# Reordering the attention half of a fused adaLN, linear-attention and GeGLU kernel

## The chip, the cores and the metric

The kernel runs on one core of a Trainium2 chip. The metric is the device time of one execution in microseconds; the time before the change is the median of three runs, 790.18 us (786.46 to 790.93). One execution was also recorded by the hardware profiler; its span is 788.5 us, and all the views below are of that one.

## The reference

The input x has 2048 rows (tokens) of 1024. Six modulation vectors come from a condition c. Then come a linear attention with 32 heads of 32 and a gated feed-forward part with an inner width of 3584:

```python
mod = (_silu(c) @ w_mod).reshape(c.shape[0], 6, 1, -1)
sa, ca, ga, sb, cb, gb = (mod[:, 0], mod[:, 1], mod[:, 2], mod[:, 3], mod[:, 4], mod[:, 5])
h = _layernorm(x) * (1 + ca) + sa
q, k, v = h @ wqkv                      # split in 32 heads of 32
phi = lambda t: where(t > 0, t + 1, exp(t)) + 1e-6
kv = einsum('bhsd,bhse->bhde', phi(k), v)
z = sum over s of phi(k)
o = einsum('bhqd,bhde->bhqe', phi(q), kv) / (einsum('bhqd,bhd->bhq', phi(q), z) + 1e-6)
x = x + ga * (o @ wo)
h = _layernorm(x) * (1 + cb) + sb
x = x + gb * ((gelu(h @ w_gate) * (h @ w_up)) @ w_down)
```

## The kernel before, in words

The rows are cut into four blocks of 512 (four tiles of 128 rows each). The kernel keeps its operands transposed, with the contracted dimension on the 128 partitions, so each block's normalised rows are stored to a scratch in HBM (`xa_scr`) and come back through a transposing load (line 593); then eight VectorE instructions (line 595) apply scale and shift. Block 0 is transposed on TensorE instead.

The products for V, Q, gate, up and down are computed with seven in place of eight half-size products (the scheme that Strassen and Winograd made known). It needs sums of operand halves, which VectorE makes beforehand (`h_sum` line 598, `w_sum` line 605, `h2_sums` line 913), and combinations of partial results afterwards. `seven` (line 629) gives the seven stages s1 to s7 of V or Q; each is 8 matmuls of 128x128 by 512 columns. The partial sums of s1, s3, s5 and s6 share two banks of the accumulator memory (`QA`), those of s2, s4 and s7 two others (`QB`). K is a plain product in groups of 8 matmuls (`k_group`, line 749), with `phi` behind each.

The attention has a linear form, so keys and values are reduced to one matrix per head. `kv_products` (line 760) multiplies a block's phi(k) with its V and its ones column, in three groups of up to three 128-wide slices (kb = 0, 1, 2); VectorE adds each to `kvzacc`. For blocks 0 to 2 all three groups are in bank 6. At the end `kv_matrix` (line 795) makes the block-diagonal matrices. `wp_step` (line 785) folds them into the output weight: Wp = KV times (Wo times ga). `den_start` (line 774) makes the denominators of one slice of 512 rows on TensorE, its reciprocal by Ln and Exp on ScalarE, and the returned function multiplies phi(q) by it on VectorE; there are 32 of those.

`ModSet` (line 465) computes the modulation vectors, in three sets of two. A set has eight `step`s, each of four 32-row matmuls on one 512 KB piece of w_mod; then `columns` copies the row out of the accumulator (line 493), turns it into columns with four small matmuls (line 498) and copies those (line 500); `spread` copies a vector over all partitions with two matmuls (line 506). These use banks 6 and 7 in turn.

`kvq_phase` writes TensorE's order out by hand: `blocks[b]` is a list of K groups, V stages and Q stages, and `put(b, i, ...)` hangs other work at position i of block b. A K group does the hung work after its matmuls; a V or Q stage does it before them. Q works on a pair of blocks at a time and on a quarter of the columns per seven stages: `Q[pr, j]`. `wo_phase` (line 936) holds the last Q stages, the Wp steps and the denominators, and then the 16 output tiles (`wo_tile`, line 922: 16 matmuls, two additions of x, and a store of the new x to `x2_scr`). The first eight tiles are layer-normed at once (`ln2_stats`, `ln2_xhat`) and come back through two transposing loads (line 901) as the operand of the first feed-forward half; `h2_mod` (line 908) scales and shifts them. `gate_up(g)` and `down_out(g)` do the feed-forward part for each half of the rows (g = 0, 1).

Every call is recorded by `Plan` and issued at the end. TensorE keeps the order of the program. The order of VectorE, ScalarE, GpSimd and the SyncE queue, which issues all loads, comes from `Plan.order`: it simulates the program forward with assumed costs, picking by due times, simulates it backward to get new due times, repeats this from two starts, and keeps the best. Each engine and the SyncE queue then does its work in that order: an instruction that waits holds up all that stand behind it. Buffers are written out by hand as offsets in one big tile; rings (`Ring`) hand out their slots in turn, and a write into a slot waits for the last readers of that memory.

Of the kernel before, what the change touches and what calls it, by code (L numbers as in the profile page):

```python
# [20 lines left out]
class Op:  # L21
    __slots__ = ("eng", "fn", "args", "kw", "line", "cost", "bytes", "table", "preds", "succs", "due", "ready", "wait",
                 "start", "done", "n")


class Plan:

    LINE = 16

# [44 lines left out]
    def add(self, eng, name, args, kw, line):  # L74
        op = Op()
        op.n, op.eng, op.fn, op.args, op.kw, op.line = len(self.ops), eng, name, args, kw, line
        op.preds, op.succs, op.bytes, op.table = set(), set(), 0, None
# [28 lines left out]
    def cost(self, op, outs, ins):  # L106
# [8 lines left out]
        elif op.fn.startswith("dma"):  # L115
            a = outs[0]
            op.cost, op.bytes = 1000 if op.eng == "POOL" else 60, math.prod(d[1] for d in a.ap) * (4 if a.dtype == FP32 else 2)
            if op.fn == "dma_start_transpose":
                op.bytes = 3584 * 360
# [16 lines left out]
    SYNC = 120  # L136
    DMA_LATENCY = 1500
    GBPS = 360
    AHEAD = 15000
    ROUNDS = 6  # L140

    def sweep(self, back, key):
# [12 lines left out]
        while left:  # L155
            best = None
            for e in self.engines:
# [5 lines left out]
                else:  # L163
                    if not avail[e]:
                        continue
                    when = lambda o: o.ready if back or not o.bytes else max(o.ready, o.due - self.AHEAD)
# [10 lines left out]
            if op.bytes:  # L177
                bw = max(bw, op.done) + op.bytes / self.GBPS
                op.done = bw + self.DMA_LATENCY
# [5 lines left out]
            for s in op.preds if back else op.succs:  # L185
                o = ops[s]
                o.wait -= 1
                o.ready = max(o.ready, op.done + (0 if o.eng == op.eng and not op.bytes else self.SYNC))
# [3 lines left out]

    def slack(self):
        t, ideal = 0.0, {}
        for op in self.ops:
            if op.eng == "PE":
                ideal[op.n] = t
                t += op.cost
        for op in reversed(self.ops):
            dur = op.cost + (self.DMA_LATENCY + op.bytes / self.GBPS if op.bytes else 0)  # L200
            due = min((self.ops[s].due - self.SYNC for s in op.succs), default=t + 20000.0) - dur
            op.due = min(due, ideal[op.n]) if op.eng == "PE" else due

    def order(self):
# [8 lines left out]
        def backward():  # L213
            t = self.sweep(True, lambda o: (-o.due, -o.n))
            for op in self.ops:
                op.due = t - op.done

        for rounds in (1, 3):
            if rounds == 1:
                self.slack()  # L220
            else:
                for op in self.ops:
                    op.due = op.n
            forward()
            if rounds == 3:
                for op in self.ops:
                    op.due = op.start
            for i in range(rounds):
                backward()
                forward()  # L230
                for op in self.ops:
                    op.due = op.start
        return [self.ops[n] for _, n in best[1]]
# [13 lines left out]
def kernel(  # L247
# [130 lines left out]
    wm0_ring.slots += Ring(170, [MW], BF16, 1).slots  # L378
# [6 lines left out]
    pqT = [pq2[0][:, 0], pq2[0][:, 1], pq2[1][:, 1], pq2[1][:, 0]]  # L385
    h12 = [at(104, [2, KD, TG], F16), at(136, [2, KD, TG], F16)]
    hr1 = [h12[0][:, 0], h12[0][:, 1], h12[1][:, 1], h12[1][:, 0]]
    WvT = at(120, [3, KH, NW], F16)
    Wp = at(120, [KD, D], F16)
    Sab = [at(152, [2, 3, KH, HB], F16), at(158, [2, 3, KH, HB], F16)]  # L390
    Sb = [Sab[0][:, 0], Sab[0][:, 1], Sab[1][:, 1], Sab[1][:, 0]]
    wm_ring = Ring(195.25, [MW], BF16, 2)
    qf_ring = Ring(170, [TG], FP32, 6)
    Wo_sb = at(11.75, [KD, D], BF16)
    phe_ring = Ring(182, [TG], F16, 3)
    phr_ring = Ring(185, [TG], F16, 3)
# [6 lines left out]
    bst_ring = Ring(205, [NBN, nc.vector.BN_STATS_DIM], FP32, 4)  # L403
# [20 lines left out]
    xio_ring = Ring(183, [NW], BF16, 6)  # L424
# [349 lines left out]
    def den_start(b, g):  # L774
# [3 lines left out]
        ac.activation(out=lnd, in_=psd, func=AF.Ln, bias=eps6, scale=1.0)  # L778
        rden = rden_ring()
# [27 lines left out]
    def kvq_phase():  # L807
# [32 lines left out]
        k, v = kk[1], V[1]  # L840
        blocks.append([k[0], k[1], v[0], k[2], v[1], k[3], v[2], k[4], v[3], k[5], v[4], k[6], v[5], k[7], v[6]])
        k, v, q = kk[2], V[2], Q[0, 0] + Q[0, 2]
# [93 lines left out]
    def wo_phase(last):  # L936
        dens = []
        for i in range(4):
            last[i](())
            for f in dens:  # L940
                f()
# [269 lines left out]
```

## Time and profile before

| | us | share of the span |
|---|---|---|
| span of the profiled run | 788.5 | |
| TensorE matmul busy (PE) | 761.5 | 97% |
| TensorE weight load busy (PEld) | 343.5 | 44% |
| VectorE busy (DVE) | 567.7 | 72% |
| ScalarE busy (ACT) | 330.1 | 42% |
| GpSimd busy (POOL) | 54.0 | 7% |
| mean traffic of HBM | 154 GB/s | |
| first matmul | at 4.87 | |
| first gate and up matmul (line 1003) | at 275.76 | |
| last VectorE instruction begins | at 785.34 | |

A line of a group of instructions names its line in the kernel, the engine, the operation, the output and input with their shapes, and a count; after the first bar come the busy time and the mean duration in ns, after the second the time for which the engine stood idle just before, and what ended it. A line of the waits names the instruction that waited, then what it waited for, the total, how often, and the longest. "PE psum L754 <- DVE mem L595" is TensorE's matmul of line 754 waiting for the VectorE instruction of line 595. The duration of one matmul in the trace includes its way through the array; the pace of a stream of matmuls is read from one start to the next.

### The profile page before, as it was taken

To read this page: it belongs to the slowest core of one execution; us is meant where nothing else is said; L and a number is where in the kernel's file an instruction comes from. 1 tells how busy PE (TensorE), PEld (TensorE's weight loads), DVE (VectorE), ACT (ScalarE), POOL (GpSimd) and SP (SyncE) were. 2 spreads that over 40 slices of the span, in tenths; PEclk is the share of its full clock that TensorE was granted. 3 is DMA by queue.
4 is the path that set the end of the run, shared out by engine and by line. 5 is a ranking of instruction groups with operands and counts; after the bars stand their busy time and mean duration, and the time that the engine had idled before them with its cause. 6 is when DMAs were issued, how large, how long until landed. Compare 5 with 4: busy or idle time off the path is not lost.

```text
span 788.5 us, 10345 instructions
## 1 busy us (share of the span) xinstructions
PE 761.5 (97%) x3666; PEld 343.5 (44%) x3666; DVE 567.7 (72%) x1145; ACT 330.1 (42%) x575; POOL 54.0 (7%) x120
## 2 busy tenths in 40 slices
PE   5989998999999999999999999999999999999997
PEld 2434443444344444444444444444444444444443
DVE  4996756748997987788897677597777677646144
ACT  1764645846994055454445301004454454530000
POOL 1221200000034100000000014000000000000000
PEclk9999999999999999999999999999999999999999
DMA  9957663003149943366666789952313323356561
GB/s 334 332 138 210 224 189 68 2 14 120 41 134 266 247 141 87 100 184 204 226 194 247 269 286 305 303 172 67 107 56 105 105 56 107 98 185 197 174 207 47
DMA packets 147155, 129.12 MB, mean 164 GB/s; under 512 B 34977, under 2 KB 127649, under 8 KB 147105
## 3 DMA queue, kind: packets, MB, share of 16 engines
q1 hardware_dynamic: 138976, 112.74, 47.5%
q0 software_dynamic: 3520, 11.54, 4.0%
q10 hardware_dynamic: 4608, 4.20, 1.6%
q8 instruction: 28, 0.46, 0.2%
q14 instruction: 23, 0.18, 0.1%
HBM read 98.04 MB, written 23.07 MB: 154 GB/s over the span
## 4 chain that ended last, share of the span: by engine, by line
PE 79%; DVE 10%; DMA 7%; issue 1%; SPq 1%; ACT 0%; POOL 0%; DVEq 0%; POOLq 0%
PE psum L1003 43%; PE psum L1105 21%; DVE mem L463 5%; PE psum L754 4%; PE psum L693 4%; PE psum L721 4%; DMA mem<-in_A_wqkv_dram 3%; DVE mem L512 2%; DMA mem<-xas 1%; DMA mem<-xhs 1%; DMA mem<-in_A_x_dram 1%; DMA mem<-in_w_mod_dram 1%; PE psum L765 1%; SPq L456 1%; DVE mem L791 1%
## 5 line engine op out<-in xcount | busy, mean ns | idle before, releaser
L1003 PE MATMUL psum<-mem 128*128 128x512 f16 x1568 | 338.9, 379 | 0.4 <-DVE mem L463 0.4
L463 DVE TENSOR_TENSOR mem<-psum,mem 128x512 f16<-128x512 f32 (+3 forms) x285 | 191.0, 680 | 73.2 <-PE psum L1003 35.1
L1003 PEld LDWEIGHTS <-mem 128*128 128x128 f16 (+1 forms) x1568 | 153.4, 98 | 185.6 <-issue 0.7
L626 ACT ACTIVATE mem<-psum 128x512 f32<-128x512 f32 x232 | 136.2, 594 | 226.0 <-PE psum L1003 142.5
L463 DVE TENSOR_TENSOR mem<-mem 128x512 f16<-128x512 f16 (+6 forms) x398 | 200.1, 532 | 27.7 <-DMA mem<-in_B_w_up_dram 10.9
L1105 PE MATMUL psum<-mem 128*128 128x512 f16 (+1 forms) x784 | 169.5, 379 | 0.0
L1105 PEld LDWEIGHTS <-mem 128*128 128x128 f16 x784 | 76.7, 98 | 92.5
L1015 ACT ACTIVATE mem<-mem 128x512 f16<-128x512 f16 x84 | 52.9, 629 | 98.7 <-DVE mem L463 98.6
L754 PE MATMUL psum<-mem 128*128 128x512 bf16 x256 | 61.0, 386 | 4.6 <-DVE mem L595 3.1
L930 PE MATMUL psum<-mem 128*128 128x512 f16 x256 | 57.5, 379 | 2.1 <-DVE mem L463 1.9
L721 PE MATMUL psum<-mem 128*128 128x512 f16 x224 | 52.7, 388 | 0.0
L693 PE MATMUL psum<-mem 128*128 128x512 f16 (+1 forms) x224 | 52.2, 379 | 0.0
L512 DVE BATCH_NORM_STATS2 mem<-mem 128x6 f32<-128x512 bf16 x64 | 41.9, 675 | 2.2 <-DMA mem<-in_A_x_dram 1.9
L754 PEld LDWEIGHTS <-mem 128*128 128x128 f16 x256 | 25.0, 99 | 36.2 <-DVE mem L595 5.0
L930 PEld LDWEIGHTS <-mem 128*128 128x128 bf16 x256 | 24.9, 98 | 33.2 <-issue 3.0
L614 ACT ACTIVATE mem<-psum 128x512 f16<-128x512 f32 x40 | 23.8, 595 | 35.5 <-PE psum L754 33.9
L721 PEld LDWEIGHTS <-mem 128*128 128x128 f16 (+1 forms) x224 | 21.8, 99 | 27.8 <-issue 4.5
L693 PEld LDWEIGHTS <-mem 128*128 128x128 f16 x224 | 20.8, 98 | 26.9 <-issue 3.9
L1117 DVE TENSOR_TENSOR mem<-psum,mem 128x512 f16<-128x512 f32 x24 | 16.5, 687 | 19.9 <-PE psum L1105 19.9
L619 DVE TENSOR_SCALAR mem<-mem 128x512 f16<-128x512 f16 x56 | 15.9, 286 | 19.3 <-ACT mem L614 19.1
L519 POOL TENSOR_SCALAR mem<-mem 128x1 f32<-128x1 f32 x28 | 8.3, 296 | 270.2 <-DVE mem L514 270.1
L616 ACT ACTIVATE mem<-psum 128x512 f16<-128x512 f32 x40 | 23.8, 596 | 0.0
(86 smaller groups left out, 364.8 us busy)
## 6 DMA issues: line engine op xcount, KB each, us to landing
mem<-in_B_w_gate_dram SPq DMA_DIRECT2D x28, 512.0 KB, 3.9
mem<-in_B_w_up_dram SPq DMA_DIRECT2D x28, 512.0 KB, 5.2
mem<-ts SPq DMA_DIRECT2D x112, 128.0 KB, 3.1
mem<-in_w_mod_dram SPq DMA_DIRECT2D x24, 512.0 KB, 5.0
mem<-in_B_w_down_dram SPq DMA_DIRECT2D x6, 1792.0 KB, 7.7
mem<-in_A_x_dram SPq DMA_DIRECT2D x32, 256.0 KB, 4.0
mem<-in_B_w_down_dram SPq DMA_DIRECT2D x14, 512.0 KB, 6.6
ts<-mem SPq DMA_DIRECT2D x14, 512.0 KB, 3.6
```

Source lines behind the costliest of these rows:

```text
L463: ve.tensor_tensor(out=out, in0=a, in1=b, op=op)
L512: ve.bn_stats(out=stats[:, cb, :], in_=xt[:, cb * BW:(cb + 1) * BW])
L614: ac.activation(out=e, in_=t, func=AF.Exp)
L616: ac.activation(out=r, in_=t, func=AF.Relu)
L626: ac.activation(out=t, in_=ps, func=AF.Copy)
L693: te.matmul(ps, lhsT=A[:, k, i * P:(i + 1) * P], rhs=B[:, k, :], start=(start and k == 0), stop=(k == KH - 1), skip_group_check=True)
L721: te.matmul(o, lhsT=W[:, k, (j0 + i) * P:(j0 + i + 1) * P], rhs=h_form(a, k), start=(start and k == 0), stop=(k == KH - 1), skip_group_che ...
L754: te.matmul(ps, lhsT=hr1[b][:, k, tl * P:(tl + 1) * P], rhs=Wk[:, k, n * NW:(n + 1) * NW], start=(k == 0), stop=(k == KD - 1))
L930: te.matmul(psw, lhsT=pqT[b][:, g, tl * P:(tl + 1) * P], rhs=Wp[:, g, cs], start=(g == 0), stop=(g == KD - 1))
L1003: te.matmul(ps, lhsT=a[:, u, k, :], rhs=b[:, k, :], start=(start and k == 0), stop=(k == KH - 1), skip_group_check=True)
L1015: ac.activation(out=t, in_=src, func=AF.Gelu_apprx_tanh)
L1105: te.matmul(ps, lhsT=a[:, i, q * P:(q + 1) * P], rhs=b[:, i, :], start=(start and i == 0), stop=(i == NPR - 1), skip_group_check=True)
```

## The change

It changes the order of the work in the attention half, four details of the planner, some buffer addresses and the end of `down_out`. It is meant to take TensorE's waits out of the attention half and to shorten the tail.

- Planner: one start (program order) with five forward sweeps instead of two starts; in the backward sweep a hop between engines counts as 300 ns and not 120; due times are taken against the best time so far; only loads, not stores, are held back until 15 us before they are due.
- Orders set by hand after the planner: gate and up loads of the first unit right after the load of Wo; the first transposing load of the second layer norm after the tenth x load; the scaling of its second half (eight instructions) after the third addition of the output tiles from there; the first Ln of the denominators eight places earlier on ScalarE.
- TensorE's order: blocks 1 to 3 share one pattern of K groups and V stages, with `Q[0, 0]` in block 2 and `Q[0, 2]` in block 3; Wq's load, the steps, columns and spreads of the modulation sets sit at other positions.
- A `merge_phase` takes `Q[1, 0]` and `Q[1, 2]` (14 stages), the last key-value products, the matrices, the gating of Wo, the eight Wp steps and eight denominators; `wo_phase` keeps the tiles and the other 24 denominators, three to a tile.
- Buffers: the sums of blocks 1 and 3 no longer share memory, and several rings move; the ring of output tiles in `down_out` has eight slots and not six.
- `down_out`: in the last group of products the residual is loaded, and gating and addition to the partial sum are done, before the last matmuls; the very last tile is done in two halves of 256 columns.

```diff
     def backward():
             t = self.sweep(True, lambda o: (-o.due, -o.n))
             for op in self.ops:
-                op.due = t - op.done
+                op.due = min(t, best[0]) - op.done
...
+        gate, up = (self.ops[n] for n in self.wl[0:2])
+        t0, t1 = (self.ops[n] for n in self.tr[0:2])
+        wo = next(op for op in seq if op.fn == "dma_start" and op.eng == "SP" and op.n == self.wo[0])
+        for op in (up, gate):
+            seq.remove(op)
+            seq.insert(seq.index(wo) + 1, op)
+        xl = [op for op in seq if op.n in self.xl]
+        seq.remove(t0)
+        seq.insert(seq.index(xl[9]) + 1, t0)
+        h1 = [self.ops[n] for n in self.mods[8:16]]
...
+        after = [op for op in ve[k:] if op.n in self.adds][2]
...
+        k = ac.index(ln0)
+        ac.remove(ln0)
+        ac.insert(k - 8, ln0)
...
-        k, v = kk[1], V[1]
-        blocks.append([k[0], k[1], v[0], k[2], v[1], k[3], v[2], k[4], v[3], k[5], v[4], k[6], v[5], k[7], v[6]])
-        k, v, q = kk[2], V[2], Q[0, 0] + Q[0, 2]
-        blocks.append([k[0], k[1], v[0], k[2], v[1], k[3], v[2], v[3], k[4], v[4], v[5], k[5], v[6], q[0], q[1], k[6],
-                       q[2], q[3], k[7]] + q[4:])
-        k, v, q = kk[3], V[3], Q[1, 0]
-        blocks.append([k[0], k[1], v[0], k[2], v[1], k[3], v[2], k[4], v[3], k[5], v[4], k[6], v[5], k[7], v[6]] + q)
+        for b in range(1, NG):
+            k, v, q = kk[b], V[b], Q[0, 2 * b - 4] if b >= 2 else []
+            blocks.append([k[0], k[1], v[0], k[2], k[3], v[1], v[2], k[4], v[3], v[4], k[5], v[5], v[6], k[6]] +
+                          q[:2] + [k[7]] + q[2:])
...
-        put(1, 12, F(load_w, Wq, 0))
+        put(1, 10, F(load_w, Wq, 0))
...
         for i in range(KD):
             put(1, 2 * i, ms1.step)
-            put(2, 4 + 2 * i, ms2.step)
-        put(2, 0, ms1.columns)
+            put(2, 3 + 2 * i, ms2.step)
+        put(2, 1, ms1.columns)
         put(2, 2, F(ms1.spread, 0, garow, GA_SCALE))
-        put(2, 19, ms2.columns)
-        put(2, 21, F(ms2.spread, 2, gbrow, 1.0),
+        put(2, 20, ms2.columns)
+        put(3, 5, F(ms2.spread, 2, gbrow, 1.0),
...
-        return Q[1, 2]
+        return Q[1, 0] + Q[1, 2]
...
+    def merge_phase(stages):
+        sy.dma_start(out=Wo_sb, in_=A_wo.rearrange("(kd p) n -> p kd n", p=P))
+        plan.wo.append(len(plan.ops) - 1)
+        for i, stage in enumerate(stages):
+            if i < NKB:
+                kv_products(NG - 1, i)
+            if i == 4:
+                kv_matrix(1)
+                kv_matrix(0)
+            if 4 <= i < 4 + KD // 2:
+                for kd in (2 * i - 8, 2 * i - 7):
+                    tt_op(Wo_sb[:, kd, :].bitcast(F16), Wo_sb[:, kd, :], garow, ALU.mult)
+            if 6 <= i < 6 + KD:
+                den_start(*den_todo.pop(0))()
+                wp_step(i - 6)
+            stage(())
...
         for tt in range(NTT):
-            for f in dens:
-                f()
-            dens = [den_start(*den_todo.pop(0)) for _ in range(min(3, len(den_todo)) if tt else 2)]
+            for _ in range(min(3, len(den_todo))):
+                den_start(*den_todo.pop(0))()
             xt = wo_tile(tt, psX if tt < 4 else psC)
-            if tt < 3:
-                last[4 + tt](())
-            if xhat is not None:
-                ln2_xhat(*xhat)
-                xhat = None
             if tt < 2 * TT:
-                xhat = (tt, xt) + ln2_stats(xt)
+                ln2_xhat(tt, xt, *ln2_stats(xt))
...
             t = f32_ring()
-            ve.tensor_tensor(out=t, in0=pa[q], in1=p5[q], op=ALU.add)
-            w12.append(t)
+            tt_op(t, pa[q], p5[q], ALU.add)
+            w12.append((t,) + rest(q, 1))
+            _, cs, xt = w12[q][1:]
+            tt_op(t, t, gbrow[:, cs], ALU.mult)
+            tt_op(t, t, xt, ALU.add)
...
         for q in range(TT):
-            ps = psB()
-            mm_f(ps, A12, q, wd, True)
-            finish(q, 1, ps, w12[q])
+            y, tt, cs, xt = w12[q]
+            parts = 2 if (g, q) == (NGR - 1, TT - 1) else 1
+            for n in range(parts):
+                ps = psB()
+                c = slice(n * NW // parts, (n + 1) * NW // parts)
+                mm_f(ps[:, c], A12, q, wd[:, :, c], True)
+                t = c0_ring()[:, c]
+                tt_op(t, ps[:, c], gbrow[:, cs][:, c], ALU.mult)
+                tt_op(xt[:, c], t, y[:, c], ALU.add)
+                ac.dma_start(out=o_dram[tt * P:(tt + 1) * P, cs][:, c], in_=xt[:, c])
```

## The prediction

> **What bounds the kernel now.** I read the page first, then PE's own waits, then PE's stretch by stretch, then what the engine that ended each wait was doing. The page:
>
> ```profile
> PE 761.5 (97%) x3666; PEld 343.5 (44%) x3666; DVE 567.7 (72%) x1145; ACT 330.1 (42%) x575; POOL 54.0 (7%) x120
> ...
> L1003 PE MATMUL psum<-mem 128*128 128x512 f16 x1568 | 338.9, 379 | 0.4 <-DVE mem L463 0.4
> ...
> L1105 PE MATMUL psum<-mem 128*128 128x512 f16 (+1 forms) x784 | 169.5, 379 | 0.0
> ```
>
> TensorE is the bound, and two thirds of its time is the feed-forward part (L1003, L1105), which waits for nothing: 2352 matmuls from 275.8 to 784 us, 0.216 us each. The change can't shorten that. What is left is the 275 us ahead of it and the 4.3 us behind it. Ahead of it I count at the pace of this trace (0.216 us for a matmul of 512 columns, 0.058 for one of 129, 0.0825 for one of 32 rows): some 242 us of TensorE work, done between 4.9 and 275.8 us. So 28 us are lost there. TensorE's waits say where:
>
> ```profile
> PE psum L754 <- DVE mem L595: 3.1, 1, 3.1
> PE psum L498 <- DVE mem L493: 3.0, 2, 2.8
> PE psum L765 <- DVE mem L463: 2.1, 2, 1.3
> PE psum L930 <- DVE mem L463: 1.9, 3, 1.0
> ...
> PE psum L776 <- DVE mem L791: 1.6, 6, 0.5
> ...
> PE psum L765 <- DVE mem L770: 0.7, 1, 0.7
> ```
>
> Nearly all end on VectorE. The two long ones, in TensorE's timeline (start, length, engine, line, count, wait before it):
>
> ```profile
> 51.09 3.33 PE L754 MATMUL psum<-mem 128*128 128x512 bf16 x8 [3.09 <-DVE mem L595]
> ...
> 128.26 0.25 PE L498 MATMUL psum<-mem 128*128 128x4 f16 x4 [2.77 <-DVE mem L493]
> 128.38 5.30 PE L721 MATMUL psum<-mem 128*128 128x512 f16 x16
> ```
>
> The reader should see the second price: after 51.09 eight matmuls take 3.33 us and not 1.73; after 128.38 sixteen take 5.1 and not 3.45. The pauses cost 4.7 and 4.5 us, not 3.1 and 2.8. What VectorE did ahead of the second:
>
> ```profile
> 125.26 2.35 DVE L595 TENSOR_SCALAR mem<-mem 128x512 f16<-128x512 f16 x7 [4.05 <-DMA mem<-xas]
> 127.52 0.68 DVE L493 CAST mem<-psum 128x512 f16<-128x512 f32 x1
> ```
>
> It stood 4.05 us for a transposed load, scaled block 3's rows, which nobody needed yet, and only then made the copy (L493) TensorE was waiting for: a head-of-queue block. Last, the stretch from the end of block 3 to the feed-forward part, and the tail:
>
> ```profile
> 180.00:200.00 20.00, 18.24 (x103) 8.66 (x102) 19.59 (x42) 14.09 (x26) 0.00 (x0) 1.00 0.25 82
> 200.00:220.00 20.00, 18.85 (x85) 7.99 (x84) 19.04 (x44) 19.51 (x36) 2.63 (x5) 1.00 0.15 52
> 220.00:240.00 20.00, 20.00 (x94) 9.04 (x93) 19.75 (x49) 19.24 (x36) 7.63 (x15) 1.00 0.49 160
> ...
> 784.16 0.69 DVE L1117 TENSOR_TENSOR mem<-psum,mem 128x512 f16<-128x512 f32 x1 [1.41 <-PE psum L1105]
> 784.88 0.42 DVE L1118 TENSOR_TENSOR mem<-mem 128x512 f16<-128x512 f16 x1
> 785.34 0.42 DVE L1119 TENSOR_TENSOR mem<-mem 128x512 bf16<-128x512 f16 x1
> ```
>
> Columns after the length: PE, PEld, DVE, ACT, POOL busy, clock, DMA share, GB/s. From 180 to 240 VectorE is full, from 200 ScalarE too. This is where the change rebuilds most.
>
> **What the Trainium skill says.** "TensorE: Matmul & The Clock Gate", in "What's actually happening" of Part 1: an idle window of about 3.4 us halves the array's clock until a busy window has passed. The trace agrees in kind (granted clock 0.66 in 50 to 55 us, 0.75 in 130 to 135), and here waits of 2.77 and 3.09 us were enough. "Perfetto Trace Analysis", "Matmuls": independent groups should rotate through banks so one's evacuation lies beside the next one's matmuls. The trace agrees: the key-value products, all in one bank, wait 0.65 to 1.31 us on the third group; the seven Q stages, on two pairs of banks, don't wait. "VectorE: DVE Perf Modes", "The perf-mode tier table": a tensor-tensor op from PSUM or in fp32 runs at 1x, 16-bit from SBUF at 2x. The trace: 0.68 against 0.42 us at 512 elements.
>
> **The change part by part.**
>
> (A) Key-value products. Before, the second group (position 3, after K's matmuls) and the third (position 4, ahead of V's) follow each other with nothing between, in one bank, so the third waits for VectorE to empty the second. Now a K group, 1.73 us, lies between. It removes the waits at 62.5, 95.6 and 157.0: 0.65 + 1.31 + 0.80 = 2.76 us. The 1.31 had its cause in a weight load that held VectorE, so a rest may stay: I take -2.5 (bounds -1.5 and -2.8).
>
> (B) The third modulation set's columns. Before at position 19, straight after its last step at 18; now at 20, its last step at 17, so three Q stages (5.2 us) lie between. The copy alone takes 0.68. That pays back 2.77 + 1.7 us of slow clock: -4.5 (bounds 0, if VectorE's queue blocks again, and -4.5).
>
> (C) New bank conflicts. The second set's columns move from position 0 to 1, now right behind a key-value group in the same bank 6: TensorE must wait for the 0.56 us evacuation and about 0.2 us of signalling, then the second spread waits for the columns' copy (about 0.35), where before one wait of 0.56 stood. Behind it are the V stages of block 2. The third set's spread at position 5 of block 3 also follows a group in bank 6: about 0.5. Sum +1.1 (bounds +0.5, +3).
>
> (D) Merge and output projection. Before, the second pair's first seven Q stages ran with the key-value products, the other seven with the Wp steps and the first tiles. Now all 14 stages, the matrices, 16 Wp products and the first 8 denominators are one phase, one denominator and one Wp step to a stage. TensorE: 14 x 1.73 + 16 x 0.216 + 8 x 0.216 + 32 x 0.058 + 0.6 = 31.8 us. VectorE, with the time from one start to the next (0.60 for a PSUM op, 0.33 for a 16-bit one, 0.20 for a scalar one): Q 2 x 8.4, products 1.3, matrix 1.15 + 0.65 + 1.3, gating 8 x 0.60, Wp 12 x 0.60, denominators 8 x 0.33: 35.8 us. ScalarE: Q 2 x 10.2, denominators 8 x 1.1, Wp 2: 31 us. So VectorE is over by 4 us; two can slide beneath the first tiles, where a tile with its layer norm and three denominators is 4.0 us of VectorE against 4.1 of TensorE. Against it stand the losses of now: from 176.5 to 275.8 TensorE does 92.2 us of work in 99.3, so 7.1 are lost. The smaller bursts (3 banks of 4 per stage, before 6 at once) end the L776 waits. The x load ahead of the transposed load, the gate and up loads moved to the front of the queue, and the additions ahead of the second half's scaling answer the waits at 257.2 (1.03, VectorE 3.98 us idle on an x load behind a transpose whose issue held the queue 7.2 us) and 266.9 (0.69). I leave 3.6 of the 7.1: -3.5 (bounds +2: VectorE's 4 us in full and the transposed load that much later; -6).
>
> (E) Tail. Before, three VectorE ops follow the last matmul: 784.16 to 785.76, 1.60 us. Now gating and the residual are added to the partial sum earlier, leaving two ops, on half a tile: 256 elements from PSUM, (256 + 151) / 0.96 = 0.42 us by the formula in that VectorE page's errata section (it gives 0.69 for 512, as here), and one in fp32 alike, so 0.34 + 0.40 = 0.75. -0.85, and about 0.15 on a store of 64 and not 128 KB: -1.0. The split itself is free: 28 matmuls of 256 columns at about 0.108 us are as long as 14 at 0.216, and a 0.098 us weight load fits under each. The fp32 ops that prepare it (8 per half at 0.6 us) hide under the matmuls of L1105, where VectorE is 7 to 9 us busy in 20.
>
> (F) The order of the other engines. The planner starts from program order alone, counts 300 ns per hop in its backward pass, and lets stores go when ready. TensorE's order is fixed by the program, so this matters only where VectorE or a queue is late. The case is the 4.7 us at 51: the transposed load was issued at 44.46, after the last row store at 42.0, after row statistics that had three weight sums ahead of them (36.3 to 38.1). A longer back hop pulls that chain forward; nothing in the trace says by how much. Bounds 0 and -4.7; I take 0. The moved Ln on ScalarE, the bank pairs of block order and the new addresses: nothing, they hide under TensorE or touch buffers that are free by then.
>
> Sum: -2.5 - 4.5 + 1.1 - 3.5 - 1.0 = -10.4; 790.2 - 10.4 = 779.8.
>
> **Rivals.** (1) VectorE becomes the bound of the merge phase: D is +2 in place of -3.5, 785. For it: 35.8 against 31.8 us, and a VectorE already at 19.0 to 19.75 of 20. Against: before, the same work at the same fullness cost TensorE only some 3 us. (2) The new order also ends the wait at 51 and D comes near its bound: -4.7 and 2 more, 773. For it: the chain there was held by work that could wait. Against: in 0 to 35 us the DMA engines are full, and the x rows come late anyhow. (3) Slower: the new order blocks VectorE's queue on a transposed or weight load at two other places, each with the clock drop (4.5 us each), and the merge phase loses its 4 us and its gain: 779.8 + 9 + 5.5 = 794. For it: exactly such a block caused the wait at 128, and C puts a bank wait near the Wq load that landed at 94.4. Against: A, B and E are by program order, not by the planner.
>
> **How the numbers follow.** Forecast 0.52, rival 1 0.20, rival 2 0.18, rival 3 0.10. The range 769 to 787 holds the forecast with the bounds of C and F, and rivals 1 and 2; rival 3 and the ends of the others are left out. Faster by over 0.5% (under 786.2): forecast and rival 2 nearly whole, most of rival 1, 0.86. Within 0.5%: 0.06. Slower: 0.08.
>
> **What would show it.** A: no wait of the key-value products (L765) over 0.3 us. B: no stretch between 100 and 150 us with a clock under 1. C: short waits of the columns' and the spread's matmuls. D: TensorE waits between the end of block 3's Q stages and the feed-forward part summing to about 3 us, with VectorE over 19 of 20 in the merge phase. E: last matmul to the end 3.3 us. F: the wait at 51 as before. The feed-forward part stays 508 us; if it differs, my account is wrong. A new wait of over 2.5 us on TensorE, with its clock drop, would undo half of the gain.

## The result, and the profile after

The kernel after takes 780.46 us (median of 12 runs, 777.94 to 784.43), the one before 788.77 (15 runs beside it): the ratio is 0.9906, with a 95% interval of 0.9885 to 0.9926. So the change brings 7.4 us by the ratio (5.8 to 9.1), or about 8.3 by the medians; forecast were 10.4 us and a time of 779.8. The profiled execution has a span of 780.0 us, against 788.5.

The time came out close to the forecast, the gain less so: the 15 runs of the kernel before have a median 1.4 us under the 790.18 of three runs from which the forecast started, and 10.4 us lie outside the measured gain's interval. Nor did the forecast's sum hold: one term that was counted at -3.5 us brought nothing, and one that was counted at nothing brought about two. First the page of the kernel after:

```profile
span 780.0 us, 10390 instructions
...
PE 760.5 (98%) x3680; PEld 344.8 (44%) x3680; DVE 571.6 (73%) x1155; ACT 330.6 (42%) x575; POOL 55.3 (7%) x120
...
L1032 PE MATMUL psum<-mem 128*128 128x512 f16 x1568 | 339.1, 379 | 1.2 <-DVE mem L500 1.1
...
L1134 PE MATMUL psum<-mem 128*128 128x512 f16 (+2 forms) x798 | 169.6, 375 | 0.0
```

The feed-forward part is the same work at the same pace (339.1 and 169.6 us; its lines are now L1032 and L1134). All that changed lies ahead of it and behind it. TensorE's waits after (who waited, for whom, total, times, longest):

```profile
PE psum L827 <- DVE mem L829: 2.7, 1, 2.7
...
PE psum L957 <- DVE mem L500: 1.6, 3, 1.0
PE psum L1032 <- DVE mem L500: 1.1, 1, 1.1
PE psum L535 <- DVE mem L500: 0.7, 1, 0.7
PE psum L791 <- ACT mem L653: 0.6, 1, 0.6
PE psum L543 <- DVE mem L537: 0.4, 1, 0.4
PE psum L543 <- DVE mem L500: 0.3, 1, 0.3
```

Gone are the 3.1 us of the first K group of block 1 (line 754, now 791), the 2.8 us of the third set's columns (498, now 535), those of the key-value products (765, now 802) and of the denominators (776, now 813). New is one wait of 2.7 us at the second half of a Wp step (line 827), which before stood nowhere. The places of the old waits, in TensorE's timeline after (start, length, engine, line, count, wait before it in brackets, where there is one):

```profile
49.59 2.65 PE L791 MATMUL psum<-mem 128*128 128x512 bf16 x8
...
87.33 0.24 PE L535 MATMUL psum<-mem 128*128 128x4 f16 x4 [0.69 <-DVE mem L500]
...
88.16 0.38 PE L543 MATMUL psum<-mem 128*128 128x512 f16 x1 [0.35 <-DVE mem L537]
...
94.67 0.63 PE L802 MATMUL psum<-mem 128*128 128x129 f16 x8
...
124.09 0.24 PE L535 MATMUL psum<-mem 128*128 128x4 f16 x4
```

The lines at 49.59, 94.67 and 124.09 have no bracket: these waits have ended. One loss is left at the first: its eight matmuls take 2.58 us to the next start (52.17) and not 1.73, at a full clock. Each waits for one of the eight scalings of its operand (line 632), which VectorE makes in one row from 49.14 to 51.79, one every 0.32 us. Those at 87.33 and 88.16 are the new bank conflicts that the prediction's part (C) named. And the new wait, in the same view:

```profile
183.65 0.38 PE L827 MATMUL psum<-mem 128*128 128x512 f16 x1
186.73 0.59 PE L827 MATMUL psum<-mem 128*128 128x512 f16 x1 [2.70 <-DVE mem L829]
187.11 3.22 PE L758 MATMUL psum<-mem 128*128 128x512 f16 x8
190.17 0.38 PE L813 MATMUL psum<-mem 128*128 128x512 bf16 x1
```

The eight matmuls behind it take 3.06 us from 187.11 to 190.17 and not 1.73: the slow clock again, here after 2.70 us. The Wp matmul behind the wait loses another 0.16, so the wait costs 2.70 + 1.33 + 0.16 = 4.2 us. What VectorE did meanwhile:

```profile
181.54 0.68 DVE L500 TENSOR_TENSOR mem<-psum,mem 128x512 f16<-128x512 f32 x1
182.72 0.29 DVE L656 TENSOR_SCALAR mem<-mem 128x512 f16<-128x512 f16 x1 [0.50 <-ACT mem L651]
182.93 1.62 DVE L500 TENSOR_TENSOR mem<-mem 128x1024 f16<-128x1024 bf16 x3
184.47 0.28 DVE L656 TENSOR_SCALAR mem<-mem 128x512 f16<-128x512 f16 x1
184.86 0.42 DVE L500 TENSOR_TENSOR mem<-mem 128x512 bf16<-128x512 f16 x1
185.20 0.28 DVE L656 TENSOR_SCALAR mem<-mem 128x512 f16<-128x512 f16 x1
185.40 0.68 DVE L500 TENSOR_TENSOR mem<-psum,mem 128x512 f16<-128x512 f32 x1
186.00 0.68 DVE L829 TENSOR_SCALAR mem<-psum 128x512 f16<-128x512 f32 x1
```

The matmul of the first Wp step that wrote the bank began at 181.28; VectorE begins to empty it (L829) at 186.00. Between them stand a wait of 0.50 us for ScalarE, phi (three of L656 and one sum of L500), three gatings of Wo (the 1.62) and a Q sum. The four banks 4 to 7 serve the transposes of the matrices, the denominators and both halves of a Wp step in turn, so the second step's second half comes back to the bank of the first step's first half and waits for that instruction. The 20 us windows (PE, PEld, DVE, ACT and POOL busy, granted clock, DMA share, GB/s):

```profile
180.00:200.00 20.00, 17.30 (x74) 7.52 (x73) 19.18 (x43) 17.63 (x34) 0.00 (x0) 0.91 0.14 40
200.00:220.00 20.00, 19.29 (x89) 8.48 (x87) 19.75 (x46) 19.87 (x38) 2.56 (x5) 1.00 0.12 41
```

Where the time went, from the two timelines. Rows are stretches of the prediction's parts; a minus is a gain.

| part | forecast, us | measured, us | from |
|---|---|---|---|
| A key-value products | -2.5 | -2.8 | waits of 0.65, 1.31 and 0.80 gone |
| B third set's columns | -4.5 | -4.5 | wait of 2.77 and 1.7 of slow clock gone |
| C bank conflicts | +1.1 | +1.4 | 0.69 + 0.35 + 0.30 less 0.56 before, and 0.58 of line 791 on ScalarE, which is no bank conflict |
| D merge and output projection | -3.5 | +0.2 | start of merge to first gate and up matmul 99.3 then, 98.8 now; a wait of 1.08 just behind, 0.4 then |
| E tail | -1.0 | -0.95 | last read of a bank to the end: 788.5 - 784.16 = 4.35 then, 780.0 - 776.61 = 3.4 now |
| F order, wait at 51 us | 0 | -2.2 | end of block 1's first K group 54.35 then, 52.17 now |

The sum is -8.85 us; the spans differ by 8.5. A, B and C together can be read apart from the list: from 54.35 to the start of the merge phase at 176.46 it was 122.1 us, from 52.17 to 168.41 it is 116.2, which is -5.9, as the three rows say. The places that bound these stretches, in TensorE's timeline before:

```profile
54.35 0.40 PE L485 MATMUL psum<-mem 128*32 128x512 bf16 x4
...
176.46 1.89 PE L721 MATMUL psum<-mem 128*128 128x512 f16 x8
```

And after (the first key-value products of the merge phase, the denominators behind its last stage, the first gate and up matmuls):

```profile
168.41 0.86 PE L802 MATMUL psum<-mem 128*128 128x129 f16 x12
...
204.41 0.81 PE L813 MATMUL psum<-mem 128*128 128x512 bf16 x3
...
267.22 7.35 PE L1032 MATMUL psum<-mem 128*128 128x512 f16 x32
```

The merge phase, from 168.41 to 204.41, takes 36.0 us: TensorE's own work of 31.8, and the 4.2 of the new wait. In this stretch VectorE is busy for 34.92 us and ScalarE for 29.85.

### The profile page after: what moved, and what is told of

Read it like the earlier page. It is cut to its first block, busy times and chain, and to the rows that moved or that the text cites. A ratio compares the mean times of both kernels' runs of the same rounds, so it can differ in the third digit from the quotient of the medians.

```text
span 780.0 us, 10390 instructions
## 1 busy us (share of the span) xinstructions
PE 760.5 (98%) x3680; PEld 344.8 (44%) x3680; DVE 571.6 (73%) x1155; ACT 330.6 (42%) x575; POOL 55.3 (7%) x120
## 4 chain that ended last, share of the span: by engine, by line
PE 87%; DVE 7%; DMA 2%; ACT 2%; issue 1%; DVEq 0%; SPq 0%
PE psum L1032 43%; PE psum L1134 22%; PE psum L791 6%; PE psum L758 6%; PE psum L957 4%; DVE mem L500 4%; PE psum L730 4%; DVE mem L549 2%; DMA mem<-xas 1%; DMA mem<-in_A_x_dram 1%; PE psum L572 1%; PE psum L522 1%; PE psum L802 1%; ACT mem L815 0%; PE psum L813 0%
## 5 line engine op out<-in xcount | busy, mean ns | idle before, releaser
L1032 PE MATMUL psum<-mem 128*128 128x512 f16 x1568 | 339.1, 379 | 1.2 <-DVE mem L500 1.1
L500 DVE TENSOR_TENSOR mem<-psum,mem 128x512 f16<-128x512 f32 (+3 forms) x302 | 201.7, 679 | 123.0 <-ACT mem L663 63.7
L1032 PEld LDWEIGHTS <-mem 128*128 128x128 f16 (+1 forms) x1568 | 153.4, 98 | 186.5 <-issue 1.8
L500 DVE TENSOR_TENSOR mem<-mem 128x1024 f16<-128x1024 bf16 (+8 forms) x423 | 213.9, 539 | 14.8 <-issue 1.8
L1134 PE MATMUL psum<-mem 128*128 128x512 f16 (+2 forms) x798 | 169.6, 375 | 0.0
L1134 PEld LDWEIGHTS <-mem 128*128 128x128 f16 x798 | 78.1, 98 | 91.4
L730 PE MATMUL psum<-mem 128*128 128x512 f16 (+1 forms) x224 | 51.1, 379 | 0.0
L656 DVE TENSOR_SCALAR mem<-mem 128x512 f16<-128x512 f16 x56 | 15.9, 284 | 17.1 <-ACT mem L651 16.9
L815 ACT ACTIVATE mem<-psum,mem 128x512 f32<-128x512 f32 x32 | 20.9, 686 | 2.3 <-PE psum L813 2.2
```

What stands on the lines that cost most here:

```text
L500: ve.tensor_tensor(out=out, in0=a, in1=b, op=op)
L730: te.matmul(ps, lhsT=A[:, k, i * P:(i + 1) * P], rhs=B[:, k, :], start=(start and k == 0), stop=(k == KH - 1), skip_group_check=True)
L1032: te.matmul(ps, lhsT=a[:, u, k, :], rhs=b[:, k, :], start=(start and k == 0), stop=(k == KH - 1), skip_group_check=True)
L1134: te.matmul(ps, lhsT=a[:, i, q * P:(q + 1) * P], rhs=b[:, i, :], start=(start and i == 0), stop=(i == NPR - 1), skip_group_check=True)
```

## The experiments

Each is the kernel after with one edit, save where it says the kernel before. Ratios are to the kernel before, run beside it; in these terms the kernel after is 0.9906.

**The new wait of the merge phase: its cause.** Four kernels. The first puts the hand-moved Ln back to the planner's place:

```diff
-        ac.insert(k - 8, ln0)
+        ac.insert(k, ln0)
```

> The first Ln of the denominators stays where the planner put it on ScalarE; nothing else moves. Theory (VectorE's backlog makes TensorE wait 2.7 us in the merge phase): the wait of the second Wp step stays at 2 us or more, and the time within 1.5 us of the changed kernel's 780.5. Rival (ScalarE, which stood 1.35 us for the moved Ln and so gave its Exp results late to VectorE): the wait and its slow clock go, about -4 us.

It took 781.51 us, 0.9896 (0.9865 to 0.9926). TensorE's timeline:

```profile
187.77 0.59 PE L827 MATMUL psum<-mem 128*128 128x512 f16 x2 [2.57 <-ACT mem L815]
188.20 1.89 PE L758 MATMUL psum<-mem 128*128 128x512 f16 x8
```

The wait stays, at 2.57; only the engine that ends it is another, the Ln (line 815) behind Exp and Relu of phi. So the move of the Ln isn't the cause. The matmuls behind run at full pace here (1.73 us to the next start), so no clock was lost.

The second narrows the eight gatings of Wo, the largest single piece ahead of L829, keeping the order of all instructions (most of the gating is left out):

```diff
             for op in self.order():
+                if op.n in self.gates:
+                    op.kw = {k: a if k == "op" else a[:, 0:64] for k, a in op.kw.items()}
```

> The eight gating instructions of Wo work on 64 and not 1024 columns, so most of Wo stays without its gate; every order is the same. VectorE has 8 x 0.55 = 4.4 us less to do in the merge phase. Theory (VectorE is the bound there): the 2.7 us wait and its slow clock go, -4 to -5 us, about 776. Rival (ScalarE or the order of the queues is the bound): the wait stays at over 2 us, and the time at 780 to 781.

It took 779.73 us, 0.9883 (0.9844 to 0.9921), no clear gain over the kernel after. TensorE still waits 2.27 us at 185.97, and 0.46 at 191.12. VectorE's timeline (its lines are three further down):

```profile
180.47 0.68 DVE L503 TENSOR_TENSOR mem<-psum,mem 128x512 f16<-128x512 f32 x1
182.39 0.29 DVE L659 TENSOR_SCALAR mem<-mem 128x512 f16<-128x512 f16 x1 [1.24 <-ACT mem L654]
182.60 0.83 DVE L503 TENSOR_TENSOR mem<-mem 128x64 f16<-128x64 bf16 x3
...
185.24 0.68 DVE L832 TENSOR_SCALAR mem<-psum 128x512 f16<-128x512 f32 x1
```

Of the time saved on gating, 1.24 us became a wait on ScalarE, at the head of VectorE's queue. VectorE is now busy for only 31.39 of the merge phase's 34.70 us, and TensorE's waits there are as long in sum as before (2.73 us). My theory of a VectorE backlog through the gating fell with this. The third run relieves ScalarE in its place: Exp and Relu of phi in the merge phase on 64 of 512 columns (the rest is left out), the order the same:

```diff
+    def slim(self, o): o.kw = {k: a[:, 0:64] if k in ("out", "in_") else a for k, a in o.kw.items()} if o.n in self.phis else o.kw; return o
...
-            for op in self.order():
+            for op in [self.slim(o) for o in self.order()]:
```

> In the merge phase the Exp and Relu of phi(q) work on 64 and not 512 columns, so most of phi(q) of the second pair of blocks is left out; every order and every other instruction is the same. ScalarE has some 8 us less to do there. Theory now (ScalarE's late phi results hold VectorE's queue, and that holds the emptying of the Wp banks; narrower gates on VectorE alone took only 0.4 us off the wait): the wait of about 2.7 us at the second Wp step falls under 1 us and the clock stays full, -3 to -4 us, 777. Rival (four banks shared by transposes, denominators and Wp are the bound whatever the engines do): the wait stays at about 2 us.

It took 779.42 us, 0.991 (0.9893 to 0.9927), and the wait is 2.33. VectorE has no wait ahead of L829 (here L830) now, and as much work ahead of it as before; its timeline:

```profile
181.37 0.68 DVE L501 TENSOR_TENSOR mem<-psum,mem 128x512 f16<-128x512 f32 x1
182.02 0.29 DVE L657 TENSOR_SCALAR mem<-mem 128x512 f16<-128x512 f16 x1
182.22 1.62 DVE L501 TENSOR_TENSOR mem<-mem 128x1024 f16<-128x1024 bf16 x3
...
185.30 0.68 DVE L830 TENSOR_SCALAR mem<-psum 128x512 f16<-128x512 f32 x1
```

This fell too; its rival, four shared banks as the bound whatever the engines do, had expected a wait of about 2 us. Each relief alone takes about 0.4 us off the wait (2.70 to 2.27 and 2.33). That fits two chains of nearly equal length into the same instruction, one over ScalarE's phi and one of VectorE's own work, but it isn't shown, for both runs keep a third thing: VectorE's order, in which L829 stands behind phi, gatings and a sum. In the kernel after, the matmul that filled the bank had ended by 181.7, and VectorE stood idle from 182.22 to 182.72 for ScalarE's phi, with L829 behind it. An estimate from these times: L829 ahead of that phi would have emptied the bank at about 182.9 (0.68 us later), 1 us before TensorE came back to it at about 183.9. No run tries this order.

The fourth spreads the work out: block 3's key-value products three positions earlier, the matrices at stage 1 and not 4, the gating from stage 2:

```diff
+        for kb in range(NKB):
+            put(3, 19 + kb, F(kv_products, 3, kb))
...
-            if i < NKB:
-                kv_products(NG - 1, i)
-            if i == 4:
+            if i == 1:
...
-            if 4 <= i < 4 + KD // 2:
-                for kd in (2 * i - 8, 2 * i - 7):
+            if 2 <= i < 2 + KD // 2:
+                for kd in (2 * i - 4, 2 * i - 3):
```

> The last block's key-value products run at the end of block 3, the matrices at stage 1 and the gating from stage 2 of the merge phase; the work is the same. Theory (VectorE's matrix work falls just ahead of the Wp steps, makes the Q sums late, ScalarE's Exp later, and so the emptying of the banks): spread over more stages it costs no 2.7 us wait and no slow clock, -3 to -4.5 us. Rival (VectorE and ScalarE have more work in the phase than TensorE wherever it stands): the wait comes back at another Wp step, within 1.5 us of the changed kernel.

It took 781.8 us, 0.9918 (0.9884 to 0.9951): no gain. TensorE's timeline:

```profile
185.50 0.38 PE L827 MATMUL psum<-mem 128*128 128x512 f16 x1 [1.26 <-DVE mem L829]
...
187.96 0.38 PE L813 MATMUL psum<-mem 128*128 128x512 bf16 x1 [0.36 <-DVE mem L829]
189.10 0.59 PE L827 MATMUL psum<-mem 128*128 128x512 f16 x2 [0.76 <-ACT mem L815]
```

1.26 + 0.36 + 0.76 = 2.4 us: the wait is cut in three and is nearly as long in sum, on VectorE twice and ScalarE once. Only its clock drop is gone. What these four runs show is that TensorE waits for banks which VectorE, in places ScalarE, empties late, and that neither the Ln, the gating nor phi alone is the reason. Relief of both engines at once, L829 earlier in VectorE's order, and a fifth bank for the Wp steps were not tried.

**Part B alone.** The kernel before, with only the columns and their spread three positions later:

```diff
-        put(2, 19, ms2.columns)
-        put(2, 21, F(ms2.spread, 2, gbrow, 1.0),
+        put(2, 22, ms2.columns)
+        put(2, 24, F(ms2.spread, 2, gbrow, 1.0),
```

> The kernel before, with only the third modulation set's columns three positions later (22 and not 19) and its spread at 24. Theory: its 2.8 us wait and the slow clock after it go, -4.5 us against the kernel before (0.994). Rival (the planner then lets VectorE's queue block on the transposed load at another place): a wait of over 2 us elsewhere between 100 and 150 us, within 1.5 us of before.

It took 784.45 us, 0.994 (0.9918 to 0.9961): 0.006 x 788.9 = 4.7 us (3.1 to 6.5). TensorE's timeline:

```profile
131.60 0.24 PE L498 MATMUL psum<-mem 128*128 128x4 f16 x4
131.70 3.61 PE L721 MATMUL psum<-mem 128*128 128x512 f16 x16
```

No bracket, and sixteen matmuls in 3.45 us to the next start. Two changed numbers give more than half of what the whole change gives.

**Part A, and what the hand orders bring.** First the planner's own sequence, without the orders set by hand behind it; then that same kernel with the second and third group of key-value products next to each other again:

```diff
-        seq = [self.ops[n] for _, n in best[1]]
+        return [self.ops[n] for _, n in best[1]]
```

> All four orders set by hand are left out; TensorE's order is the same. Theory: they are worth 1 to 2 us, mostly at the two waits of the last tiles and of the first feed-forward matmuls, so 781.5 to 782.5, and the 2.7 us wait in the merge phase stays. Rival (the moved Ln costs more than the other three bring): 777 to 779, without that wait.

```diff
-            for kb, i in enumerate((1, 3, 4)):
+            for kb, i in enumerate((1, 4, 5)):
```

> The changed kernel without the orders set by hand, and with the second and third group of key-value products next to each other again (positions 4 and 5), in one bank. To be compared with the run without hand orders. Theory: three waits of 0.6 to 1.3 us come back in front of the third groups, +2 to +3 us. Rival (the one-bank waits were due to VectorE's weight loads only): at most one wait, under +1 us.

The first took 786.69 us, 0.996 (0.9942 to 0.9977); beside it on the same chip, the kernel with only the Ln put back has 0.9896, so the other hand orders are worth about 0.0064 x 790 = 5 us, more than the 1 to 2 us that I expected. The place, in TensorE's timeline of the first:

```profile
259.98 13.12 PE L957 MATMUL psum<-mem 128*128 128x512 f16 x48 [4.63 <-DVE mem L500]
```

VectorE there stood 6.43 us, until 257.94, for a transposed load whose rows were not needed yet, while additions of the output tiles that TensorE waited for stood behind: the head-of-queue block of the kernel before in another place. With its slow clock (the 48 matmuls take 13.0 us to the next start, and not 10.4) it costs 7.2 us. Putting the scaling behind the third addition is made against this block; no run has that order alone.

The second took 790.26 us, 1.0012 (0.9994 to 1.003), so 0.0052 x 789 = 4.1 us more than the first. Its trace has the three waits of line 802 again (0.84, 0.79 and 0.80, together 2.4 us, as the forecast of 2.5 has it), the first at 62.25:

```profile
62.25 0.62 PE L802 MATMUL psum<-mem 128*128 128x129 f16 x8 [0.84 <-DVE mem L807]
```

The rest of the 4.1 isn't A's price: the planner put other instructions elsewhere too, which brought among others a wait of 2.4 us on ScalarE in the feed-forward part and took the 4.63 us at 260 away.

**Part F: what ended the wait at 51 us.** Only the price of a hop in the backward sweep is put back:

```diff
-    SYNC, SYNC_BACK = 120, 300
+    SYNC, SYNC_BACK = 120, 120
```

> The changed kernel with the backward pass counting 120 ns per hop as before. Theory (the 300 ns are what moved the row-statistics chain of block 1 forward and ended the 3.1 us wait before block 1's first K group): that wait comes back, with 1.5 to 3.5 us on TensorE, 782 to 784. Rival (the new start from program order or the exemption of stores did it): no wait over 1 us there, within 1.5 us of the changed kernel.

It took 789.83 us, 1.0036 (1.002 to 1.0052), as slow as the kernel before and slower than the 782 to 784 that I expected. TensorE's timeline:

```profile
51.43 1.89 PE L791 MATMUL psum<-mem 128*128 128x512 bf16 x4 [3.20 <-DVE mem L632]
```

The wait is back (3.20 us) with a clock of 0.83 from 50 to 60 us, and the transposing load is issued at 44.88, as before the change (44.46) and not as after it (42.76). So the dearer hop is what pulled block 1's statistics ahead of the weight sums: after, those of the first of block 1's rows are done at 28.3 us, in this run at 32.3, as before the change (32.3). It is not the whole of the difference, since the same number moves other instructions, too: 1.5 us at the second set's columns and 1.9 in the feed-forward part. And the profile is of this kernel's fastest execution (785.76), so some of what makes its median longer isn't in it.

**Part E: split or early gating.** The last tile in one piece, all else as after:

```diff
-            parts = 2 if (g, q) == (NGR - 1, TT - 1) else 1
+            parts = 1
```

> The last output tile in one piece of 512 columns, with gating and residual still added ahead. Theory: of the tail's 0.95 us gain the split is worth about 0.55 us: from the start of the last VectorE reading of PSUM to the end of the span about 0.4 us longer than in the changed kernel. Rival (the early gating alone gives the gain): under 0.15 us longer.

It took 783.34 us in its only run, with the wait of 2.7 us and its clock drop as in the kernel after, and further waits of 0.9 us in the feed-forward part. For the tail the profile is enough:

```profile
777.44 0.69 DVE L500 TENSOR_TENSOR mem<-psum,mem 128x512 f16<-128x512 f32 x1 [1.60 <-PE psum L1134]
778.17 0.69 DVE L500 TENSOR_TENSOR mem<-mem 128x512 bf16<-128x512 f16 x1
```

From 777.44 to the end at 781.6 it is 4.16 us; in two halves it is 3.4 (the two instructions take 0.42 each there), before the change 4.35. So the split brings some 0.75 of the 0.95 us, more than the 0.55 that I expected, and the gating ahead of time 0.2: it removes one of three instructions, but the second, with an fp32 operand, takes 0.69 in place of 0.42.

**The waits at the last output tiles.** In the kernel after, TensorE waits 1.00 us at 260.32 and 1.08 at 275.65, and VectorE stands 4.52 us, until 259.57, for rows of x that the queue loads between two transposing loads. Is it the queue, or the DMA engines? One kernel issues these x loads from ScalarE's queue:

```diff
-        sy.dma_start(out=xt, in_=x_in[tt * P:(tt + 1) * P, :])
+        (ac if tt >= 12 else sy).dma_start(out=xt, in_=x_in[tt * P:(tt + 1) * P, :])
```

> The x loads of the last four output tiles are issued from ScalarE's queue and not from SyncE's, where they stand behind the second transposing load; every compute order is the same. Theory (the queue holds them up): VectorE's 4.5 us wait for x goes, the wait of 1.0 us at the last tiles with it, and the 1.1 us one in the first feed-forward matmuls shrinks: -1.5 to -2 us. Rival (the DMA engines are full there, so the loads land no earlier, or the transposing load lands later by as much): within 0.5 us.

It took 783.99 us, 0.9946 (0.9925 to 0.9966): no gain, and rather slower than the kernel after. VectorE's timeline:

```profile
260.46 1.29 DVE L500 TENSOR_TENSOR mem<-psum,mem 128x512 bf16<-128x512 f32 x2 [5.70 <-DMA mem<-in_A_x_dram]
```

A load issued at 250.12, 1.2 us behind the transposing load, landed at about 260.4, 10.2 us later, where the median x load takes some 3: its own queue was free, so the queue isn't what held it. That it is the DMA engines, which then carried the transposing load, fits their busy share of 1.1 to 1.6 from 252 to 260 us. The other kernel gives these x rows a ring of eleven slots and not four, so that all of them load ahead of both transposing loads; the scaling of the second half stands where the planner put it:

```diff
-        seq.insert(seq.index(xl[9]) + 1, t0)
+        seq.insert(seq.index(xl[9]) + 1, t0); [(seq.remove(op), seq.insert(seq.index(t0), op)) for op in xl[10:]]
...
-        first = [op for op in h1 if ve.index(op) < ve.index(after)]
+        first = [op for op in h1 if False]
...
-    x2_ring = Ring(191, [D], BF16, 4)
+    x2_ring, xw_ring = Ring(191, [D], BF16, 4), Ring(191, [D], BF16, 4); xw_ring.slots += Ring(144, [D], BF16, 7).slots
...
-        xt = x2_ring()
+        xt = xw_ring()
```

> The x rows of the output tiles get eleven slots and not four, so that all sixteen x loads stand and land ahead of both transposing loads; the scaling of the second half stays where the planner put it. Theory (an x load beside a transposing load lands only after it, whichever queue issues it, because of the DMA engines): VectorE's 4.5 us wait for x and TensorE's waits of 1.0 and 1.1 us go, -2 us, 778 to 779; the wait in the merge phase stays. Rival (the first feed-forward matmuls wait for the second transposing load in any case): the waits move to the first feed-forward matmuls, within 0.5 us of the changed kernel.

It took 779.11 us, 0.9879 (0.9851 to 0.9906), with a span of 777.1 us. The queue of the loads and, from another view, the stretch of the last tiles (columns as above):

```profile
230.76 2.21 SPq L951 DMA_DIRECT2D mem<-in_A_x_dram  x2
236.08 15.63 SPq L925 DMA_TRANSPOSE mem<-xhs  x2
```

```profile
240.00:260.00 20.00, 20.00 (x95) 9.05 (x93) 17.75 (x41) 1.15 (x2) 5.32 (x10) 1.00 0.97 277
```

TensorE is busy for all of the 20 us (19.32 in the kernel after), and the waits at the last tiles and at the start of the feed-forward part are gone. The wait in the merge phase is 2.1 us and costs no clock; the planner put L829 one place earlier there, ahead of a Q sum. It is the best version measured, though its interval overlaps that of the kernel after.

Both ideas in one kernel, this and the earlier matrices:

```diff
+        for kb in range(NKB):
+            put(3, 19 + kb, F(kv_products, 3, kb))
...
-        xt = x2_ring()
+        xt = xw_ring()
```

> Eleven x slots and the earlier matrices together. Theory: the gains add: the waits at the last tiles and the first feed-forward matmuls stay away, the merge phase's waits are in pieces without a slow clock; 777 to 779, ratio to before 0.985 to 0.988. Rival (the matrices give nothing beyond the clock's luck): as with the slots alone, 0.988.

It took 780.51 us, 0.992 (0.9906 to 0.9933). I was wrong: the gains don't add. The merge phase has 1.1 + 0.7 + 0.6 us of waits, as in the kernel with the early matrices alone, and 0.7 came back in the feed-forward part.

## Why the prediction was right, and where it was not

- **A and B were right in mechanism and size.** Work between the writer of a bank and the next user of that bank hides the evacuation. B was shown alone (4.7 us for 4.5 forecast), A by putting its waits back (2.4 us of waits for 2.5). B's price rests on the second cost, the slow clock behind a wait.
- **C was right in kind**: its conflicts cost 0.8 us for 1.1. A wait of 0.58 us on ScalarE at 84 us was not in the forecast.
- **D failed.** The step that failed is "VectorE is over by 4 us; two can slide beneath the first tiles", and from it "I leave 3.6 of the 7.1". The totals were about right (VectorE 34.92 us busy in the merge phase for 35.8 counted), but nothing slid: the phase took 36.0 us, 4.2 over TensorE's own work, all of it at the second Wp step. There matrices, gating, phi and Wp meet within 5 us, the four banks come round once, and TensorE stands 2.70 us and loses 1.5 of clock, which the sum of each engine's work can't see. With the tiles behind it, the stretch lost 98.8 - 92.2 = 6.6 us, against 7.1 before. I had named the warning myself ("A new wait of over 2.5 us on TensorE, with its clock drop, would undo half of the gain"); it undid all of D. The first rival, VectorE as the bound with +2, came nearer than the forecast, and the phase was as long as VectorE's sum; but with 3.5 us less of VectorE's work the waits stayed at 2.73 us, so the sum alone isn't the reason. What the runs leave standing is the late emptying of a bank; whether both engines' load, VectorE's order or the number of banks makes it late stays open.
- **D's second part was right in what to look at, too hopeful in size.** The hand orders other than the Ln bring 5 us against the planner's own sequence, where one block on the scaling cost 7.2 (which of the orders bring how much was not run), but the x load between two transposing loads still cost 4.5 us of VectorE and about 2 of TensorE.
- **E was right in sum**: -0.95 for -1.0. The two instructions take 0.88 us from first start to last end for 0.75 counted, and the shorter store gives the rest.
- **F was taken at 0 and brought 2.2.** The step was "nothing in the trace says by how much", and the rival with -4.7 said how it could. It ended the wait and the slow clock, which brought 3.95 us (from the start of block 0's V stages to the end of block 1's first K group it was 18.89 us, it is 14.94), but block 0's V stages begin 1.8 us later than before (at 37.23 and not 35.46), so about half was paid for. Its cause was shown by the single number in the planner. The -4.7 was also too much to hope for: the prediction put the slow pace behind the wait down to the clock alone, but the scalings of line 632 hold the same eight matmuls at 2.58 us with a full clock, so about 0.85 of the 1.6 us would have stayed.

So the time was right by luck: D was 3.7 us too good, F 2.2 too bad, and the start from 790.18 was 1.4 too high. The gain was forecast 2 to 3 us too large.

## What to carry to other kernels

Ahead of each matmul that enters a bank, look at what last wrote it and where the instruction that empties it stands in its engine's queue; put an independent group of matmuls between. A phase priced by each engine's sum can still stall at one burst: count the work in each in-order queue between the moment a bank is written and the instruction that frees it (here 4.7 us from 181.28 to 186.00, for an instruction of 0.68). A plain load that is needed soon is best landed before a transposing load starts: here one issued 1.2 us behind it took 10.2 us, from another queue, too. And take the time before from enough runs: three were 1.4 us off here, a sixth of the gain.

## What the runs showed of the hardware that was not expected

The slow clock isn't tied to one length of wait. "TensorE: Matmul & The Clock Gate" of the Trainium skill, in "What's actually happening" of Part 1, gives an idle window of about 3.4 us; in these runs 2.04, 2.29, 2.70, 2.77, 3.09 and 3.20 us were followed by the slow clock (2.04 in two kernels), and 2.10, 2.27, 2.33, 2.43 and 2.57 us were not. So the measurement goes below the page's figure, and a wait between 2 and 2.6 us can cost some 1.5 us more or nothing. Nor is it tied to the kernel: the one slow stretch of the kernel after gives its profiled execution a mean clock of 0.998, and of its twelve runs three have 1.000 and one 0.995; of forty runs of the kernel before, one has 1.000 (785.65 us) and two 0.991 (794.88 and 795.49 us). What decides it stays open.

Two transposing loads issued one behind the other held the queue for 15.63 us, and nothing was lost by it, as all else that was needed had landed.
